# Retention scan and sorted experts on one core: values scaled two steps ahead, loads issued earlier, the first expert chosen sooner, the tail's order changed

## The chip, the cores and the metric

One core of one Trainium2 chip runs the whole program. The metric is the device time of one execution in microseconds. The kernel before took 504.29 us (median of 3 runs, 504.11 to 505.67). All times below are of that kernel.

## What is computed

Two stages. The first is a linear attention with decay (retention), 4 batches x 8 heads x 768 positions x 64 channels; the second sends each of the 3072 resulting rows of 512 channels through the one of 8 experts that scores highest.

```python
for t in range(S):
    state = gamma * state + einsum('bhd,bhe->bhde', k[:, :, t], v[:, :, t])
    y[:, :, t] = scale * einsum('bhd,bhde->bhe', q[:, :, t], state)
x = y.transpose(0, 2, 1, 3).reshape(B * S, H * D)
logits = x @ w_gate
e_idx = argmax(logits, axis=1)
gate_w = softmax(logits)[arange(N), e_idx]
eom = sigmoid(x @ w_output_gate)
for e in range(E):
    mask = e_idx == e
    h = maximum(x[mask] @ w1[e], 0.0)
    out[mask] = gate_w[mask, None] * eom[mask, e, None] * (h @ w2[e])
```

## The kernel before, in words

The scan is cut into 12 steps (`NP`; `LAST` is 11) of 256 positions of one batch, two chunks of 128 each. Positions are taken in order, so after step j the first 256 (j+1) rows exist. The order of TensorE, ScalarE (ACT), VectorE (DVE), GpSimd (POOL) and SyncE (SP) is written out by hand (line 198): each engine runs its instructions in the order of the program text, and waits only for what it needs.

`load(j)` (L220) issues the DMAs of q, k and v of a step on SP: `qn`, `kn` and `vn`, 1.5 MB, into buffers that later hold expert weights (`whi`, eight buffers, for k and v; `wlo`, eight, for q). `prep_v(j)` (L271) multiplies the values of a step by the decay on POOL and writes `vs` (three buffers). In step j TensorE does: the products of the masked scores `am` with `vs[j]` (`values`), the state sums of step j+1 (`sums`, from `vs[j+1]` and `kn[j+1]`), copied to SBUF by ScalarE (`copy_s`), reads of the state with q (`read`), the turning of k and q of step j+2, the scores of step j+1 (`scores`), which VectorE masks at the end of the step (`masked`, L326), and the passage of the finished rows of step j-1 to token order, with the gate products (`tokens`, L388).

Each step also routes the rows of two steps before: VectorE finds the best expert (`route1`, L408), TensorE counts (`count`, L466), VectorE works out each row's place (`route2`, L481) and its gate (`gate1`, `gate2`), ScalarE writes the scaled rows (`rows`, L456), POOL adds row numbers (`marks`, L450) and sends the rows to their places in a sorted DRAM table `srt` by two indirect DMAs (`scatter`, L518), a step later.

To begin the experts early, a first expert is picked when the counts of `PICK` + 1 steps are known (`choose`, L537; `chosen`, L542, loads its number into a register of SP). Its first 256 rows (`HEAD`), which stand in the table after step 7 (`EARLY`; if there are fewer, `early` sets `late`, and the rows are done at the kernel's end by the odd blocks), are loaded by `head_load` (L553), split into a high and a low part by `head_prep` (L563), and run through this expert while the scan ends: a generator (`head_all`, L606) yields after each matmul, and `run_head(n)` (L625) places the next n of them, 12 for the first product of a slice of weights (`head_stage1`, L578) and 12 for the second. The weights come in slices: `load_weights(s)` (L149, three buffers `raw`, one of them shared with the loaded rows) and `split_weights(s)` (L160: high part by ScalarE, low part by two subtractions, one on VectorE, one on POOL for the first eight slices).

After step 11 VectorE ranks the experts by their totals (the order chain, L857 to L884) and sends pad rows (`pads`, L886); the rest of the first expert's rows is loaded when all rows have landed (`load_x`, L942, waits for `settled`), and the expert stage (L1046) runs the remaining rows, then the seven other experts, slice by slice: 12 matmuls for `stage1`, 12 for `stage2`. There the order of VectorE, ScalarE and SP is left to the compiler; TensorE's and POOL's is written out.

The start of a step of the loop:

```python
if j >= 2:
    load(j + 3) if j + 3 < NP else None
if j == 7:
    chosen()
for s in w_at.get(j, ()):
    load_weights(s)
if j >= 3:
    scatter(j - 3)
if j > 1:
    prep_v(j + 1)
```

Of the kernel before, what the change touches and what calls it, by code (L numbers as in the profile page):

```python
# [10 lines left out]
F32 = mybir.dt.float32  # L11
# [20 lines left out]
def retention_moe_kernel(  # L32
# [14 lines left out]
    nc = tc.nc  # L47
# [7 lines left out]
    NDC = DM // P  # L55
    NF = DF // P
# [103 lines left out]
    def split_weights(s: int):  # L160
        raw = raws.pop(s)
        hi = wpool.tile([P, 2, DM], F32R, name="whi", tag="whi")
        lo = wpool.tile([P, 2, DM], F32R, name="wlo", tag="wlo")

        def perm(t):

            return t[:, 1].rearrange("p (dc a j) -> p a dc j", a=4, j=32)

        r2 = raw[:, 1].rearrange("p (a dc j) -> p a dc j", a=4, j=32)
        nc.scalar.copy(hi[:, 0], raw[:, 0])  # L170
        nc.scalar.copy(perm(hi), r2)  # L171
        nc.vector.tensor_sub(lo[:, 0], raw[:, 0], hi[:, 0].bitcast(F32))  # L172
        (nc.gpsimd if s < NF else nc.vector).tensor_sub(perm(lo), r2, perm(hi).bitcast(F32))
        wts[s] = (hi, lo)
# [15 lines left out]
    with ExitStack() as actx:  # L190
# [341 lines left out]
        PICK = 4  # L532
# [30 lines left out]
        def head_prep(g):  # L563
# [12 lines left out]
            (nc.gpsimd if g else nc.vector).tensor_sub(hd["xl"][:, 2 * g:2 * g + 2], tp, hd["xh"][:, 2 * g:2 * g + 2].bitcast(F32))  # L576

        def head_stage1(f):  # L578
# [3 lines left out]
            for r, ls in (("xh", (hi, lo)), ("xl", (hi,))):  # L582
                for dc in range(NDC):
                    for l in ls:
                        nc.tensor.matmul(ps, l[:, 0, dc * P:dc * P + P], hd[r][:, dc], start=(n == 0), stop=(n == 3 * NDC - 1))
                        n += 1
                        yield
# [4 lines left out]
            hd["h", f] = h  # L592

# [107 lines left out]
        w_at = {7: (0,), 8: (1, 2), 9: (3,)}  # L701
        s_at = {8: (0,), 9: (1,)}

        for j in range(1, LAST - 1):
            if j >= 2:
                load(j + 3) if j + 3 < NP else None
            if j == 7:
                chosen()
            for s in w_at.get(j, ()):
                load_weights(s)  # L710
            if j >= 3:
                scatter(j - 3)
            if j > 1:
                prep_v(j + 1)
# [42 lines left out]
            if j >= 2:  # L757
                rows(j - 2)
            tokens(j - 1, 2)
# [4 lines left out]
        scatter(j - 3)  # L764
        prep_v(j + 1)
        head_load()
        for s in (4, 5):
            load_weights(s)
# [13 lines left out]
        split_weights(2)  # L782
# [6 lines left out]
        copy_y(j)  # L789
        gate2(j - 2)  # L790
        route2(j - 2)
        tokens(j - 1, 2)
# [7 lines left out]
        copy_x(j - 1, 1)  # L800
        route1(j - 1)
        marks(j - 1)
        gate1(j - 1)
        tokens(j, 2, st_all)
        split_weights(3)

        j = LAST
        for s in (6,):
            load_weights(s)
# [7 lines left out]
        gate2(j - 2)  # L817
        copy_x(j - 1, 0)
        copy_x(j - 1, 1)
        head_prep(0)  # L820
        issue(read(j, 0, 1), read(j, 1, 0))
        copy_y(j)
        head_prep(1)
        route2(j - 2)
        scatter(j - 3)
        rows(j - 2)
        scatter(j - 2)
        hd["ps"] = pair(1, "h0")
# [5 lines left out]
        gate2(j - 1)  # L834
# [3 lines left out]
        route2(j - 1)  # L838
        run_head(12)
        route1(j)  # L840
        marks(j)
        rows(j - 1)
        scatter(j - 1)
        split_weights(4)
        load_weights(7)
        gate1(j)
# [8 lines left out]
        run_head(24)  # L855
# [12 lines left out]
        nc.vector.tensor_scalar(out=ck, in0=cr, scalar1=1.0 / E, scalar2=float(SLOTS), op0=ALU.mult, op1=ALU.min)  # L868
        ef8 = sm.tile([P, E], F32, name="ef8", tag="ef8")
# [24 lines left out]
        split_weights(6)  # L894
# [3 lines left out]
        settled = list(sent)  # L898
        nc.vector.tensor_copy(n_pad, cum[:, E:E + 1])
# [7 lines left out]

        no = sm.tile([P, 1], F32, name="no", tag="no")
# [12 lines left out]
        split_weights(7)  # L921
# [277 lines left out]
```

## Time and profile before

| what | us |
|---|---|
| median of 3 runs | 504.29 |
| the profiled execution | 505.92 |
| its span | 503.9 |
| TensorE busy (matmuls) | 429.4 |
| VectorE busy | 256.4 |
| ScalarE busy | 201.6 |
| GpSimd busy | 174.4 |

The span is the profiled execution without the 2.0 us around it. Engines overlap, so the busy times do not add up; PE is TensorE's matmul row. A matmul's end is modelled, so a full row means a steady stream and not TensorE at its peak. Idle time of an engine is listed with what ended it.

### The profile page before, as it was taken

Reading aid. Unit: us, or ns where it says so; the run is one execution under the profiler, and the core shown is the slowest. Engines: PE = TensorE matmul, PEld = TensorE weight load, DVE = VectorE, ACT = ScalarE, POOL = GpSimd, SP = SyncE. Lnnn points to the kernel's source line nnn. Section 1 sums busy time; section 2 is a strip of 40 time slices with the busy share of each in tenths; the row PEclk is TensorE's granted clock in tenths of the full one; section 3 lists DMA queues with packets and bytes.
Section 4 is the critical chain, followed back from the end, with each engine's and each line's share of the span. In section 5 each row is a group of like instructions: output and inputs, shape, how many; then the busy total and the mean of one; then the engine's idle time right before and its main releaser. Section 6 shows DMA issues by size and latency. Waiting matters only on the chain.

```text
span 503.9 us, 13073 instructions
## 1 busy us (share of the span) xinstructions
PE 429.4 (85%) x5117; PEld 411.1 (82%) x5119; DVE 256.4 (51%) x711; ACT 201.6 (40%) x416; POOL 174.4 (35%) x221
## 2 busy tenths in 40 slices
PE   6888867667684766769999999999999999999991
PEld 3677766666673766769999999999999999999991
DVE  2416434353542867437547547547556565575111
ACT  2345544434543545015534335335334344353111
POOL 5363233333224246203231034244144243341532
PEclk9999888879876878879999999999999999999997
DMA  9999998357113143292783384485494564841101
GB/s 171 197 239 207 254 251 187 87 141 200 32 57 86 54 161 127 86 195 85 242 203 111 125 205 132 136 220 159 129 224 144 152 192 151 209 156 40 35 24 63
DMA packets 126345, 73.88 MB, mean 147 GB/s; under 512 B 55989, under 2 KB 114873, under 8 KB 126272
## 3 DMA queue, kind: packets, MB, share of 16 engines
q1 hardware_dynamic: 119696, 59.37, 47.4%
q0 software_dynamic: 5536, 13.26, 7.6%
q8 instruction: 42, 0.69, 0.6%
q10 hardware_dynamic: 1040, 0.31, 0.4%
q14 instruction: 31, 0.25, 0.2%
HBM read 59.70 MB, written 13.70 MB: 146 GB/s over the span
## 4 chain that ended last, share of the span: by engine, by line
PE 57%; issue 13%; POOL 9%; DMA 8%; DVE 5%; SPq 4%; ACT 3%; POOLq 0%; ACTq 0%; DVEq 0%
PE h L980 23%; PE a L999 22%; PE py L313 4%; DMA srt<-row,posi 4%; POOL vs L274 3%; SPq L228 3%; POOL out_dram L177 2%; POOL srt L507 2%; PE st L313 2%; PE sc L313 1%; PE pk L301 1%; DMA gb<-in_dec_q_dram 1%; PE px L395 1%; DMA xl<-srt 1%; DMA vn<-in_v_dram 1%
## 5 line engine op out<-in xcount | busy, mean ns | idle before, releaser
L177 POOL DMA_INDIRECT out_dram<-ot,idi x84 | 82.5, 982 | 156.7 <-ACT hh L984 126.9
L980 PE MATMUL h<-xh,whi 128*128 128x224 f32 (+7 forms) x256 | 86.4, 337 | 1.6 <-issue 1.6
L999 PE MATMUL a<-hl,whi 128*128 128x224 f32 (+7 forms) x256 | 85.8, 335 | 0.5 <-DVE hl L985 0.5
L980 PE MATMUL h<-xw,whi 128*128 128x224 f32 (+7 forms) x256 | 86.1, 336 | 0.0
L980 PE MATMUL h<-xh,wlo 128*128 128x224 f32 (+7 forms) x256 | 86.1, 336 | 0.0
L999 PE MATMUL a<-hh,whi 128*128 128x224 f32 (+7 forms) x256 | 85.8, 335 | 0.3 <-ACT hh L984 0.3
L999 PE MATMUL a<-hh,wlo 128*128 128x224 f32 (+7 forms) x256 | 85.7, 335 | 0.0
L172 DVE TENSOR_TENSOR wlo<-raw,whi 128x512 fp32r<-128x512 f32 x64 | 43.9, 687 | 57.7 <-ACT whi L170 49.8
L313 PE MATMUL st<-vs,kn 64*64 64x64 f32 x704 | 39.1, 253 | 36.7 <-POOL vs L274 36.2
L985 DVE SCALAR_TENSOR_TENSOR hl<-h,hh 128x224 fp32r<-128x224 f32 (+7 forms) x64 | 35.0, 546 | 61.2 <-ACT hh L984 61.1
L313 PEld LDWEIGHTS st<-vs,kn 64*64 64x64 f32 x704 | 32.6, 161 | 40.2 <-POOL vs L274 37.9
L984 ACT ACTIVATE hh<-h 128x224 fp32r<-128x224 f32 (+7 forms) x64 | 31.0, 485 | 85.4 <-PE h L980 85.4
L170 ACT CAST whi<-raw 128x512 fp32r<-128x512 f32 x64 | 39.5, 618 | 62.3 <-PE a L999 47.2
L980 PEld LDWEIGHTS h<-xh,whi 128*128 128x128 f32 x256 | 49.0, 191 | 2.1 <-issue 1.8
L980 PEld LDWEIGHTS h<-xw,whi 128*128 128x128 f32 x256 | 49.1, 192 | 0.3
L980 PEld LDWEIGHTS h<-xh,wlo 128*128 128x128 f32 x256 | 49.0, 191 | 0.2
L999 PEld LDWEIGHTS a<-hl,whi 128*128 128x128 f32 x256 | 48.2, 188 | 1.1 <-DVE hl L985 0.7
L999 PEld LDWEIGHTS a<-hh,whi 128*128 128x128 f32 x256 | 48.2, 188 | 0.9 <-ACT hh L984 0.5
L999 PEld LDWEIGHTS a<-hh,wlo 128*128 128x128 f32 x256 | 48.2, 188 | 0.5
L369 ACT COPY sx<-st 128x256 f32<-128x256 f32 x44 | 16.4, 373 | 72.6 <-PE st L313 70.8
L507 POOL DMA_INDIRECT srt<-row,posi x24 | 25.0, 1040 | 46.1 <-DVE am L330 25.6
L171 ACT CAST whi<-raw 128x512 fp32r<-128x512 f32 x64 | 39.5, 617 | 0.0
(187 smaller groups left out, 723.6 us busy)
## 6 DMA issues: line engine op xcount, KB each, us to landing
raw<-in_moe_w_dram SPq DMA_DIRECT2D x128, 256.0 KB
qn<-in_q_dram SPq DMA_DIRECT2D x12, 512.0 KB
kn<-in_k_dram SPq DMA_DIRECT2D x24, 256.0 KB
vn<-in_v_dram SPq DMA_DIRECT2D x24, 256.0 KB
xl<-srt SPq DMA_DIRECT2D x12, 211.2 KB
xl<-srt SPq DMA_DIRECT2D x12, 195.0 KB
out_dram<-ot,idi POOLq DMA_INDIRECT x84
xl<-srt SPq DMA_DIRECT2D x4, 227.5 KB
```

Of the source, the lines that this page charges most:

```text
L170: nc.scalar.copy(hi[:, 0], raw[:, 0])
L171: nc.scalar.copy(perm(hi), r2)
L172: nc.vector.tensor_sub(lo[:, 0], raw[:, 0], hi[:, 0].bitcast(F32))
L177: st = nc.gpsimd.indirect_dma_start(out=dst, out_offset=bass.IndirectOffsetOnAxis(ap=idx, axis=0), in_=src, in_offset=None, bounds_check=n ...
L228: nc.sync.dma_start(t[:, w], chunks(src, j)[:, w * P:(w + 1) * P].rearrange("h p d -> p h d"))
L313: nc.tensor.matmul(o, l, m, start=s, stop=True, skip_group_check=True)
L369: nc.scalar.copy(t, st)
L507: ins = nc.gpsimd.indirect_dma_start(out=srt, out_offset=bass.IndirectOffsetOnAxis(ap=idx, axis=0), in_=src, in_offset=None, bounds_check= ...
L980: nc.tensor.matmul(ps[:, 0:C], l[:, 0, w], r[:, dc, 0:C], start=(n == 0), stop=(n == 3 * NDC - 1))
L984: relu = nc.scalar.activation(hh, ps[:, 0:C], AF.Relu)
L985: nc.vector.scalar_tensor_tensor(out=hl, in0=ps[:, 0:C], scalar=0.0, in1=hh.bitcast(F32), op0=ALU.max, op1=ALU.subtract)
L999: mm = nc.tensor.matmul(accs[d][:, 0:C], l[:, 1, w], r, start=(f == 0 and n == 0), stop=(f == NF - 1 and n == 2))
```

## The change

`vs` of step j+2 is made at the start of step j, ahead of the sends, where that of step j+1 was made behind them. `load(j+4)` stands where `load(j+3)` stood. The first expert is picked one step earlier, and the loads and splits of its weights move with it; for slices 4 to 7 both subtractions of a split run on VectorE. The rows of step 7 are sent at the end of step 9. The second half of the head's low part goes from POOL to VectorE. In the last two steps and in the tail `head_prep`, `gate2`, `rows`, `scatter`, the splits and the head's matmuls stand in other places; the activation and the low part behind the 12th matmul of `head_stage1` are now placed with that matmul and not with the next one.

```diff
--- before.py
+++ after.py
@@ -170,7 +170,7 @@
         nc.scalar.copy(hi[:, 0], raw[:, 0])
         nc.scalar.copy(perm(hi), r2)
         nc.vector.tensor_sub(lo[:, 0], raw[:, 0], hi[:, 0].bitcast(F32))
-        (nc.gpsimd if s < NF else nc.vector).tensor_sub(perm(lo), r2, perm(hi).bitcast(F32))
+        (nc.gpsimd if s < 4 else nc.vector).tensor_sub(perm(lo), r2, perm(hi).bitcast(F32))
         wts[s] = (hi, lo)
 
     def send(dst, idx, src, n):
@@ -529,7 +529,7 @@
             nc.vector.max_index(out=by, in_max=top, in_values=key)
             return top
 
-        PICK = 4
+        PICK = 3
         EARLY = 7
 
         hd = {}
@@ -573,7 +573,7 @@
                 dc = 2 * g + j
                 nc.vector.transpose(tp[:, j].rearrange("p (n i) -> p n i", i=32), t[:, :, dc * 32:dc * 32 + 32])
             nc.scalar.copy(hd["xh"][:, 2 * g:2 * g + 2], tp)
-            (nc.gpsimd if g else nc.vector).tensor_sub(hd["xl"][:, 2 * g:2 * g + 2], tp, hd["xh"][:, 2 * g:2 * g + 2].bitcast(F32))
+            nc.vector.tensor_sub(hd["xl"][:, 2 * g:2 * g + 2], tp, hd["xh"][:, 2 * g:2 * g + 2].bitcast(F32))
 
         def head_stage1(f):
             hi, lo = wts[f]
@@ -584,12 +584,14 @@
                     for l in ls:
                         nc.tensor.matmul(ps, l[:, 0, dc * P:dc * P + P], hd[r][:, dc], start=(n == 0), stop=(n == 3 * NDC - 1))
                         n += 1
-                        yield
+                        if n < 3 * NDC:
+                            yield
             h = hpool.tile([P, 2, HEAD], F32R, name="h0", tag="h0", bufs=3)
             nc.scalar.activation(h[:, 0], ps, AF.Relu)
             nc.vector.scalar_tensor_tensor(out=h[:, 1], in0=ps, scalar=0.0, in1=h[:, 0].bitcast(F32),
                                            op0=ALU.max, op1=ALU.subtract)
             hd["h", f] = h
+            yield
 
         def head_stage2(f):
             hi, lo = wts[f]
@@ -698,20 +700,19 @@
         load(3)
         load(4)
 
-        w_at = {7: (0,), 8: (1, 2), 9: (3,)}
-        s_at = {8: (0,), 9: (1,)}
+        w_at = {6: (0,), 7: (1,), 8: (2,), 9: (3, 4)}
+        s_at = {7: (0,), 8: (1,), 9: (2,)}
 
         for j in range(1, LAST - 1):
-            if j >= 2:
-                load(j + 3) if j + 3 < NP else None
-            if j == 7:
+            if j + 4 < NP:
+                load(j + 4)
+            if j == PICK + 3:
                 chosen()
             for s in w_at.get(j, ()):
                 load_weights(s)
+            prep_v(j + 2)
             if j >= 3:
                 scatter(j - 3)
-            if j > 1:
-                prep_v(j + 1)
             if j == 2:
                 last_consts()
             if j >= 2:
@@ -756,16 +757,15 @@
                 choose() if j - 2 == PICK else early()
             if j >= 2:
                 rows(j - 2)
+            if j == EARLY + 2:
+                scatter(j - 2)
             tokens(j - 1, 2)
             for s in s_at.get(j, ()):
                 split_weights(s)
 
         j = LAST - 1
-        scatter(j - 3)
-        prep_v(j + 1)
         head_load()
-        for s in (4, 5):
-            load_weights(s)
+        load_weights(5)
         copy_x(j - 2, 0)
         new_y(j, 0)
         av = {(w, u): values(j, w, u) for w, u in ((0, 1), (1, 1), (1, 0), (0, 0))}
@@ -779,16 +779,16 @@
         copy_s(j + 1, 1, 0)
         route1(j - 2)
         marks(j - 2)
-        split_weights(2)
         sc = scores(j + 1, 1)
         issue(sums(j + 1, 1, 0), sc[1][0:8])
         copy_s(j + 1, 1, 1)
         issue(read(j, 0, 1), read(j, 1, 0))
         gate1(j - 2)
         count(j - 2)
-        copy_y(j)
         gate2(j - 2)
         route2(j - 2)
+        copy_y(j)
+        split_weights(3)
         tokens(j - 1, 2)
         rows(j - 2)
         issue(sc[0][0:8], sc[1][8:16])
@@ -798,15 +798,16 @@
         masked(j + 1)
         copy_x(j - 1, 0)
         copy_x(j - 1, 1)
+        tokens(j, 2, st_all)
+        head_prep(0)
         route1(j - 1)
         marks(j - 1)
         gate1(j - 1)
-        tokens(j, 2, st_all)
-        split_weights(3)
+        gate2(j - 1)
+        scatter(j - 2)
 
         j = LAST
-        for s in (6,):
-            load_weights(s)
+        load_weights(6)
         new_y(j, 0)
         av = {(w, u): values(j, w, u) for w, u in ((0, 1), (0, 0), (1, 0), (1, 1))}
         issue(av[0, 1], av[0, 0])
@@ -814,36 +815,34 @@
         issue(read(j, 0, 0), read(j, 1, 1))
         touch(j)
         count(j - 2)
-        gate2(j - 2)
+        head_prep(1)
         copy_x(j - 1, 0)
         copy_x(j - 1, 1)
-        head_prep(0)
+        route2(j - 2)
         issue(read(j, 0, 1), read(j, 1, 0))
+        rows(j - 2)
         copy_y(j)
-        head_prep(1)
-        route2(j - 2)
-        scatter(j - 3)
-        rows(j - 2)
         scatter(j - 2)
+        split_weights(4)
         hd["ps"] = pair(1, "h0")
         run_head(12)
         tokens(j, 2)
         route1(j - 1)
         marks(j - 1)
         gate1(j - 1)
-        gate2(j - 1)
         copy_x(j, 0)
         copy_x(j, 1)
         count(j - 1)
         route2(j - 1)
+        gate2(j - 1)
         run_head(12)
+        rows(j - 1)
+        scatter(j - 1)
         route1(j)
         marks(j)
-        rows(j - 1)
-        scatter(j - 1)
-        split_weights(4)
+        gate1(j)
         load_weights(7)
-        gate1(j)
+        run_head(12)
         gate2(j)
         run_head(12)
         rows(j)
@@ -852,7 +851,6 @@
         totals(j)
         scatter(j)
         split_weights(5)
-        run_head(24)
 
         io_ = sm.tile([P, E], F32, name="io_", tag="io_")
         nc.vector.scalar_tensor_tensor(out=io_, in0=first, scalar=-float(16 * NT), in1=io8, op0=ALU.mult, op1=ALU.add)
@@ -866,6 +864,7 @@
         nc.vector.tensor_sub(cr, cr, ordf)
         ck = sm.tile([P, E], F32, name="ck", tag="ck")
         nc.vector.tensor_scalar(out=ck, in0=cr, scalar1=1.0 / E, scalar2=float(SLOTS), op0=ALU.mult, op1=ALU.min)
+        run_head(24)
         ef8 = sm.tile([P, E], F32, name="ef8", tag="ef8")
         nc.vector.scalar_tensor_tensor(out=ef8, in0=ordf, scalar=float(SLOTS), in1=ck, op0=ALU.mult, op1=ALU.add)
         pc = sm.tile([P, E], F32, name="pc", tag="pc")
@@ -891,11 +890,12 @@
             nc.vector.tensor_tensor(out=si, in0=sl, in1=ix, op=ALU.add)
             to_srt(si, zrow, OV, last)
 
-        split_weights(6)
         run_head(24)
         pads(pidx[:, 0:1], False)
         pads(pidx[:, 1:2], False)
         settled = list(sent)
+        split_weights(6)
+        run_head(24)
         nc.vector.tensor_copy(n_pad, cum[:, E:E + 1])
         np_ = nc.values_load(n_pad[0:1, 0:1], engines=(ET.Pool, ET.DVE), min_val=0, max_val=OV)
         with tc.If(np_ > 2 * P):
@@ -905,6 +905,8 @@
         for r in range(1, E):
             rank_e[r] = nc.values_load(order[0:1, r - 1:r], engines=(ET.SP,), min_val=0, max_val=E - 1)
 
+        split_weights(7)
+        run_head(24)
         no = sm.tile([P, 1], F32, name="no", tag="no")
         tj = sm.tile([P, E], F32, name="tj", tag="tj")
         nc.vector.tensor_scalar(out=tj, in0=cnts, scalar1=-float(SLOTS), scalar2=0.0, op0=ALU.add, op1=ALU.max)
@@ -918,7 +920,6 @@
         nc.vector.tensor_reduce(out=on, in_=ck, axis=AX.X, op=ALU.add)
         nc.vector.tensor_add(no, no, on)
         nc.vector.tensor_add(n_odd, no, late)
-        split_weights(7)
         run_head(1000)
```

## Rows read from the trace of the kernel before

A row of a timeline is: start in us, duration in us, engine, line, operation, what it writes and reads, and in brackets the engine's idle time before it with what ended that. A row of rows 2 is: from and to, length, then busy us (with the instructions) of PE, PEld (weight loads), DVE, ACT and POOL, the granted TensorE clock, the busy share of the DMA engines and GB/s. A row of rows 3 is: who waited for whom, us in total, times, the longest.

**Rows 1.** TensorE's busy tenths in 40 slices of the span

```profile
PE   6888867667684766769999999999999999999991
```

**Rows 2.** Windows: steps 4, 7, 9 and 10, the tail, the expert stage

```profile
67.53:80.86 13.33, 10.14 (x274) 9.62 (x274) 6.14 (x28) 6.17 (x14) 4.44 (x6) 0.88 1.09 240
...
109.50:124.04 14.54, 11.38 (x275) 10.54 (x275) 6.27 (x28) 6.30 (x14) 4.39 (x6) 0.81 0.92 237
...
140.89:158.29 17.40, 10.93 (x277) 10.40 (x277) 6.72 (x33) 7.49 (x17) 5.54 (x7) 0.79 0.09 32
158.29:172.13 13.84, 12.27 (x273) 11.16 (x273) 8.53 (x39) 5.86 (x16) 1.80 (x5) 0.71 0.33 80
172.13:224.04 51.91, 35.20 (x346) 33.23 (x345) 32.28 (x137) 18.33 (x45) 18.64 (x21) 0.84 0.48 139
224.04:503.90 279.86, 268.45 (x1548) 265.51 (x1548) 150.25 (x275) 109.46 (x208) 93.68 (x95) 0.98 0.49 141
```

**Rows 3.** Waits of TensorE: steps 2 to 10, then the tail

```profile
PE st L313 <- POOL vs L274: 33.4, 8, 6.7
...
PE h L585 <- DVE h L590: 8.8, 4, 4.0
```

**Rows 4.** Timeline of POOL at the edge of steps 5 and 6

```profile
84.02 0.21 POOL L454 COPY row<-ef 128x8 f32<-128x8 f32 x1 [3.08 <-DVE ef L422]
91.02 1.02 POOL L507 DMA_INDIRECT srt<-row,posi  x1 [6.79 <-DVE am L330]
...
93.36 1.91 POOL L274 TENSOR_TENSOR vs<-vn,gv 128x1024 f32<-128x1024 f32 x1
```

**Rows 5.** Timeline of TensorE, first matmul of step 6

```profile
95.33 0.37 PE L313 MATMUL st<-vs,kn 64*64 64x64 f32 x1 [3.94 <-POOL vs L274]
```

**Rows 6.** Timeline of VectorE in step 5

```profile
84.29 0.17 DVE L432 TENSOR_TENSOR j<-lg,oh 128x16 f32<-128x16 f32 x1
...
85.33 0.17 DVE L437 TENSOR_SCALAR se<-se 128x2 f32<-128x2 f32 x1
86.70 0.16 DVE L445 SCALAR_TENSOR_TENSOR den<-ez,se 128x2 f32<-128x2 f32 x1 [1.20 <-ACT ez L443]
...
89.22 1.28 DVE L330 TENSOR_TENSOR am<-sc,mask 128x512 f32<-128x512 f32 x2
```

**Rows 7.** Timelines of POOL and of VectorE in the tail

```profile
191.32 1.28 POOL L173 TENSOR_TENSOR wlo<-raw,whi 128x512 fp32r<-128x512 f32 x1
...
197.37 2.57 POOL L173 TENSOR_TENSOR wlo<-raw,whi 128x512 fp32r<-128x512 f32 x2
...
190.69 1.95 DVE L437 TENSOR_SCALAR se<-se 128x2 f32<-128x2 f32 x1
...
197.15 2.83 DVE L858 SCALAR_TENSOR_TENSOR io__3323<-first,io 128x8 f32<-128x8 f32 x1
```

**Rows 8.** Timeline of SP's DMA issues: q of steps 5 and 10

```profile
39.21 1.08 SPq L222 DMA_DIRECT2D qn<-in_q_dram  x1
...
76.85 1.17 SPq L222 DMA_DIRECT2D qn<-in_q_dram  x1
```

**Rows 9.** The costliest groups: VectorE's half of a split (line engine op, busy, mean ns)

```profile
L172 DVE TENSOR_TENSOR wlo<-raw,whi 128x512 fp32r<-128x512 f32 x64 | 43.9, 687 | 57.7 <-ACT whi L170 49.8
```

**Rows 10.** Timelines of the tail: totals, pads, load, first use, low part, expert stage

```profile
194.19 0.16 DVE L479 COPY cnts<-misc 128x8 f32<-128x8 f32 x1
...
204.64 1.00 POOL L507 DMA_INDIRECT srt<-zrow,si  x1 [4.70 <-DVE sc L889]
...
210.18 1.99 SPq L947 DMA_DIRECT2D xl<-srt  x4
...
217.05 0.17 DVE L961 CAST idi<-xl 128x7 int32<-128x7 f32 x1 [2.86 <-DMA xl<-srt]
...
219.79 0.42 DVE L590 SCALAR_TENSOR_TENSOR h<-h,h 128x256 fp32r<-128x256 f32 x1
...
224.04 0.52 PE L980 MATMUL h<-xh,whi 128*128 128x224 f32 x1 [1.58 <-issue]
```

## The prediction, made before the changed kernel ran

> **What bounds the kernel now.** I read the busy slices first, then cut the span into the twelve steps of the scan, then asked who TensorE waits for, and last followed single instructions at one step's edge. The slices show two regimes [rows 1]: in its first 18 slices TensorE is busy four to eight tenths, from then on it is full. Cut by step [rows 2], the expert stage from 224.04 to the end is 279.86 us with 268 us of TensorE work; no edit touches it, so I carry it over unchanged. What can move is the 224 us ahead of it: the steps (13 to 17 us each, only about 10 us of it TensorE work) and the tail of 51.9 us from the first matmul of step 11 to the first of the expert stage, with 35 us of TensorE work.
>
> In the steps one wait stands for nearly all of the gap: 33.4 us in 8 pieces, TensorE waiting for the scaled values `vs` [rows 3]. The order on POOL says why [rows 4]. In each step POOL first sends two row blocks of an earlier step (`srt`), which need rows that ScalarE writes at the end of the step, and only then scales the values that the next instruction of TensorE reads: sends from 91.02, `vs` at 93.36 for 1.91 us, and TensorE starts at 95.33 after 3.94 us of nothing [rows 5]. So per step I see some 10.2 us of work and one gap at its edge.
>
> **The change, part by part.**
>
> *Values two steps ahead.* `prep_v(j+2)` now stands ahead of the sends, one step earlier. Its buffer (three of them) is that of step j-1, last read in the first third of that step, so POOL can run it in the middle of step j-1, right behind `marks`, a whole step before TensorE reads it. POOL's work is unchanged: two sends, one scaling, two small copies, 4.4 to 5.5 us a step [rows 2]; nothing that feeds TensorE directly is behind it. The whole 33.4 us go. What is late next? In step 5 the masked scores end at 89.22 + 1.28 = 90.50 [rows 6], while TensorE ran out of work at 95.33 - 3.94 = 91.39 [rows 5]: 0.89 us of slack on VectorE, so TensorE itself is the next bound.
>
> *What the move costs.* The scaling leaves a moment in which VectorE had nothing to do and enters one in which it has. What that can do is seen in the tail: while POOL subtracts from 191.32 to 192.60, an instruction of VectorE of 128x2 elements takes 1.95 us; while POOL subtracts from 197.37, one of 128x8 takes 2.83 us [rows 7], and both end as POOL ends. So I bound the cost per step between nothing (it falls in VectorE's pause) and 1.91 less 0.89, 1.0 us. The new place is behind POOL's copy at 84.02 [rows 4]. VectorE's next are 84.29, then 85.33, then a pause to 86.70 in which it waits for ScalarE [rows 6]; a scaling from 84.4 to 86.3 lies mostly in that pause. I take 0.4 us, nearer the pause, for 8 steps: +3.2 us.
>
> The Trainium skill (SBUF — State Buffer, Who interferes with whom) says the port pair that the two engines share is an exclusive lock for the whole instruction, and that a VectorE instruction with two SBUF inputs contends with a GpSimd one that reads SBUF. The two rows agree with it; by that rule taken alone every step would pay 1.0 us, 8 in all instead of 3.2, which is the first rival below.
>
> *Loads four ahead.* From 39.21 to 76.85 SP issued five steps' loads, 7.5 us each [rows 8], so it already runs ahead of the steps, held by DMA and by free buffers rather than by its place in the order. Moving `load` to j+4 adds no DMA and removes none. With 10.2 us steps TensorE consumes more slowly than 7.5 us; two sends per step (0.5 MB) come between, at the 237 to 240 GB/s of steps 4 and 7 [rows 2] about 2.2 us, sum 9.7. Taken as hidden; if that cover is gone, a step is paced at up to 12 us, 1.8 more.
>
> *Choice from four steps' counts.* The register load on SP now waits one step earlier, and behind it stand the weights of the first expert and `load(11)`, as before. TensorE needs nothing of it for two steps: nothing. The counts of the reference's own inputs give the same expert (7) after four steps, with 146 rows, as after five, with 185, so the expert stage is the same.
>
> *Splits one step earlier, 4 to 7 off POOL.* A split is two casts on ScalarE and two subtractions, of 0.69 us each on VectorE [rows 9], or one there and one of 1.28 us on POOL [rows 7]. Before, POOL's half stood ahead of the sends and `vs` in two steps and made the longest waits (6.7 us [rows 3]); that is already inside the 33.4. Behind the change it is ahead of a `vs` that has a step to spare.
>
> *Clock.* TensorE's granted clock was 0.81, 0.79 and 0.71 in steps 7, 9 and 10, at times the lower of its two levels (1.2 and 2.4 GHz), and the same matmuls were 11.4, 10.9 and 12.3 us busy against 10.1 in step 4 [rows 2]. They follow the waits of rows 3. Without those I give back 3.0 of those 4.2 us.
>
> So step 11 begins 33.4 + 3.0 - 3.2 = 33.2 us earlier, at about 139.
>
> *The tail.* Two chains run through it. The order chain: totals at 194.19, pads sent from 204.64, rest of the first expert's rows loaded from 210.18, expert stage from 224.04 [rows 10]. On it the blocked 2.83 us becomes 0.17 (-2.7), as POOL has no subtraction there; split 6 goes behind the pads (-0.7) and the second half of split 5 comes onto VectorE (+0.7). Ahead of totals, the blocked 1.95 us becomes 0.17 (-1.8), and the head's low parts now leave VectorE right behind their last matmul instead of behind the next step's routing; half of `head_prep` is done a step earlier, while split 4's two subtractions and the second half of `head_prep` come on (+2.1). I take -1.0 for all this beyond the lock, between -4 (TensorE waited 8.8 us for those low parts [rows 3]) and +2. Pads: 5.5 us earlier than before, counted from step 11. From 204.64 to 224.04 it was 19.4 us: 5.5 to landing, 6.9 to the load's first use at 217.05, then the head's last low part at 219.79 behind the preparation of these rows, 2.2 of matmuls, 1.6 to the start. If the head is done by then, the stage starts some 7.8 us after the counterpart of 210.18 (6.9 and one preparation, 0.9 by estimate) instead of 13.9, 6.1 less; if its last low part stays behind the preparation, nothing. I take 2.7, just under the middle, as VectorE's order there is not written out. Tail: -8.2 us.
>
> **Sum.** The profiled execution took 505.92 us (span 503.9 and 2.0 around it), 1.6 above the median of 504.29. 505.92 - 33.2 - 8.2 = 464.5; less 1.6 it is 462.9, so **463 us**.
>
> **Rivals.**
> 1. *VectorE becomes the bound*: `vs` blocks it each step where it counts. For: rows 7. Against: the pause in rows 6. Price 1.0 a step in place of 0.4, and in steps 8 to 10, where POOL's half of a split runs just ahead, some 1.3 more each: 463 + 4.8 + 3.9 = 472. Chance 0.18.
> 2. *Loads become the bound*: 12 us in steps 3 to 8, 1.8 x 6 = 11 us: 474. Against: `load(10)`'s first part was issued at 76.85 [rows 8], before step 5 began, for use in step 8. Chance 0.07.
> 3. *The tail keeps its length*, because what POOL loses VectorE gains (two more half splits and a head part ahead of totals): 471. Chance 0.13.
> 4. *Slower*: choosing after four steps picks an expert with under 256 of the first 2048 rows. Then the flag `late` sends the kernel through the odd blocks at its end: two blocks, each with a load of its rows (6.9 us as in rows 10), one expert's 4.2 MB (17.5 us at 240 GB/s) and some 40 matmuls at the tail's 0.10 us (35.2 us for 346 [rows 2]), 4 us: an estimate of 2 x 28 = 57, so 520 us. It decides at 256: four of the eight experts have fewer by then in the reference's inputs (230 to 252), but the chosen one has 271. Chance 0.03.
> 5. *It does not do what it says*: `vs` still ends last, since a buffer or the landing of the values holds POOL until the step's end. The sends, not a buffer, ended POOL's wait in rows 4. Time as before. Chance 0.02.
>
> **Numbers.** The forecast has 0.57 and spans 455 (stage starts with the head done, no lock cost) to 471. The range to 478 takes in rivals 1 to 3 with the upper end of the lock cost. A measurement tells 0.3% (1.5 us) from no change; faster 0.95, same 0.02 (rival 5), slower 0.03 (rival 4).
>
> **What would show it.** In the changed kernel TensorE's wait for `vs` should be under 3 us in steps 3 to 10 and those steps 10 to 11 us; the masked scores should end at most 1 us after TensorE runs dry. VectorE instructions of 0.17 us that take over 1 us, beside POOL's `vs`, would show the lock, and their place whether it costs. Waits for `vn`, `kn` or `qn` by POOL, TensorE or VectorE would show rival 2. Pads should be sent some 27 us behind step 11's start (32.5 before), and the expert stage start 43 to 44 us behind it; its length should be 279 to 281 us. I am wrong if steps stay over 12 us or if the expert stage itself lengthens.

## The result and the profile after

The changed kernel took **469.92 us** (median of 4 runs, 467.40 to 472.11) beside 504.64 us for the kernel before: ratio 0.931, 95% interval 0.925 to 0.936. The forecast was 463 us in a range of 455 to 478. Two later measurements of the same kernel (e7 and e12 below) gave 466.02 us (464.20 to 466.64; ratio 0.918, 0.914 to 0.923) and 468.23 us (460.07 to 470.30). In the last of them four of six runs lie over 1.5% above the fastest and count as slow, so its ratio is left aside, and medians of all runs stand below. The profiled execution took 471.10 us, span 468.9.

TensorE's slices, beside [rows 1]: the part that is not full is 16 slices long instead of 18, and fuller.

```profile
PE   7988759789877987999999999999999999999991
```

The windows, beside [rows 2]: the nine steps 2 to 10 together, of them the longest (step 4) and a short one (step 8), then the tail and the expert stage. Columns: stretch, length, busy time (instructions) of PE, PEld, DVE, ACT, POOL, granted clock, DMA share, GB/s.

```profile
39.96:145.90 105.94, 85.81 (x2519) 78.01 (x2518) 72.07 (x270) 60.09 (x139) 43.73 (x74) 0.98 0.72 179
64.99:78.99 14.00, 10.93 (x275) 10.08 (x274) 7.30 (x28) 6.46 (x15) 5.18 (x6) 0.88 1.00 231
112.19:122.58 10.39, 9.32 (x292) 8.52 (x291) 8.26 (x29) 6.47 (x17) 5.92 (x6) 1.00 0.31 106
145.90:186.40 40.50, 32.76 (x345) 31.26 (x344) 28.15 (x146) 16.57 (x41) 11.49 (x15) 0.87 0.44 140
186.40:468.90 282.50, 270.51 (x1548) 266.94 (x1548) 152.17 (x278) 110.45 (x211) 93.97 (x95) 0.97 0.52 145
```

The same nine steps of the kernel before in one window:

```profile
39.44:172.13 132.69, 94.75 (x2520) 88.69 (x2519) 61.36 (x277) 59.72 (x139) 41.31 (x73) 0.85 0.59 144
```

Step 11 begins at 145.90 instead of 172.13, 26.2 us earlier; the tail is 40.50 instead of 51.91, 11.4 shorter; the expert stage is 282.50 instead of 279.86, 2.6 longer. Together 35.0, which is the difference of the spans (503.9 and 468.9). The nine steps hold the same 2519 matmuls (2520 in the window before, which cuts one more), yet these were busy for 85.81 us instead of 94.75, at a granted clock of 0.98 instead of 0.85. The single steps are 10.31 to 14.00 us long, and four of the nine are over 12.

TensorE's waits in the steps (36 to 146 us), beside [rows 3]. Columns: who waited for whom, us in total, times, longest.

```profile
PE py L313 <- issue: 10.3, 22, 2.0
PE sc L313 <- issue: 2.9, 2, 2.8
PE misc L472 <- DVE acc L426: 1.9, 2, 1.0
PE px L395 <- issue: 1.8, 1, 1.8
PE misc L471 <- DVE oh L424: 1.0, 2, 0.6
```

The 33.4 us for `vs` are gone. In their place stands a wait that names no other engine: "issue", time in which TensorE waited for nothing that the profile shows, 15.0 us in 25 pieces. In the kernel before it was 2.5 us over the same steps:

```profile
PE px L395 <- issue: 2.1, 2, 1.8
...
PE pq L286 <- issue: 0.2, 1, 0.2
PE py L313 <- issue: 0.2, 1, 0.2
```

POOL's timeline, beside [rows 4]: the scaling of a later step's values runs from 95.64, the sends come 6 us later, and neither holds TensorE. VectorE's timeline beside it shows what the scaling holds: an instruction of 128x8 elements that starts 0.01 us behind it takes 1.90 us and ends as it ends. The same instruction takes at most 0.17 us in the steps of the kernel before, and of all the small routing instructions there only one, in step 10 beside POOL's half of a split, takes over 0.6 us (1.25).

```profile
95.64 1.89 POOL L274 TENSOR_TENSOR vs<-vn,gv 128x1024 f32<-128x1024 f32 x1
101.84 1.47 POOL L507 DMA_INDIRECT srt<-row,posi  x1 [4.32 <-DVE am L330]
```

```profile
95.65 1.90 DVE L426 TENSOR_TENSOR acc<-acc,oh 128x8 bf16<-128x8 bf16 x1
```

The tail's timelines, beside [rows 10]: totals, pads, the load of the remaining rows, the last matmul of the head, first use of the rows, the expert stage.

```profile
164.77 0.16 DVE L479 COPY cnts<-misc 128x8 f32<-128x8 f32 x1
...
173.25 0.97 POOL L507 DMA_INDIRECT srt<-zrow,si  x1 [5.03 <-DVE sc L888]
...
178.89 0.92 SPq L948 DMA_DIRECT2D xl<-srt  x2
...
183.77 0.28 PE L603 MATMUL a<-h,wlo 128*128 128x256 f32 x1
...
185.45 0.13 DVE L962 CAST idi<-xl 128x7 int32<-128x7 f32 x1
...
186.40 0.37 PE L981 MATMUL h<-xh,whi 128*128 128x224 f32 x1 [2.35 <-ACT xh L968]
```

Pads go 27.35 us behind step 11's start (32.5 before), the load 32.99 (38.05 before), and from the load to the expert stage it is 7.51 us instead of 13.86. The head's last matmul (183.77) is done before the rows come into use (185.45), so TensorE now waits for the preparation of these rows.

### The profile page after: what moved, and what is told of

It is laid out like the page before. It is cut to its first block, busy times and chain, and to the rows that moved or that the text cites. A ratio compares the mean times of both kernels' runs of the same rounds, so it can differ in the third digit from the quotient of the medians.

```text
span 468.9 us, 13070 instructions
## 1 busy us (share of the span) xinstructions
PE 422.5 (90%) x5117; PEld 402.6 (86%) x5119; DVE 264.9 (56%) x716; ACT 201.2 (43%) x416; POOL 169.0 (36%) x216
## 4 chain that ended last, share of the span: by engine, by line
PE 48%; issue 7%; DMA 5%; DVE 4%; POOL 3%; ACT 1%; SPq 1%; POOLq 0%; DVEq 0%; ACTq 0%
PE a L1000 24%; PE h L981 24%; DMA srt<-row,posi 3%; POOL out_dram L177 3%; DMA xl<-srt 2%; SPq L948 1%; DVE xw L969 0%; ACT row L460 0%; PE h L585 0%; SPq L153 0%; DVE xt L574 0%; DVE wlo L172 0%; SPq L157 0%; DVE wlo L173 0%; DVE acc L496 0%
## 5 line engine op out<-in xcount | busy, mean ns | idle before, releaser
L172 DVE TENSOR_TENSOR wlo<-raw,whi 128x512 fp32r<-128x512 f32 x64 | 44.0, 687 | 56.6 <-ACT whi L170 46.5
L173 DVE TENSOR_TENSOR wlo<-raw,whi 128x512 fp32r<-128x512 f32 x60 | 41.0, 684 | 0.0
L313 PE MATMUL st<-vs,kn 64*64 64x64 f32 x704 | 33.2, 227 | 2.8 <-POOL vs L274 1.8
```

Of the source, the lines that this page charges most:

```text
L173: (nc.gpsimd if s < 4 else nc.vector).tensor_sub(perm(lo), r2, perm(hi).bitcast(F32))
L313: nc.tensor.matmul(o, l, m, start=s, stop=True, skip_group_check=True)
```

## The experiments

Two theories were tried for the "issue" waits: the indirect sends slow TensorE's instruction supply; or its instruction fetches are late while DMA is full. Beside them: what the single move of the values is worth, what POOL's lock on VectorE costs, and the parts that the prediction costed at nothing. Times are medians of 4 executions (e1 to e8) or 6 (e9 to e12); each run has one profile.

**e1: the values alone, on the kernel before.**

```diff
+            prep_v(j + 2)
             if j >= 3:
                 scatter(j - 3)
-            if j > 1:
-                prep_v(j + 1)
...
         scatter(j - 3)
-        prep_v(j + 1)
         head_load()
```

> The kernel before, with the scaling of the values moved two steps ahead and put ahead of the sends, and nothing else. Theory 'values': this one move carries the whole gain of the steps. TensorE's wait for vs falls from 36 us to under 4, step 11 begins 24 to 28 us earlier than 172.1, the tail keeps the length it had (50 to 53 us), so 477 to 482 us. Rival 'the early loads and the moved splits carry part of it': step 11 begins less than 18 us earlier, 486 us or more. In either case TensorE's gaps of over 0.35 us ahead of weight loads that wait on no semaphore should grow from 3.7 us in the steps to over 12, if the sends cause them and the wait for vs only hid them before.

478.48 us (476.09 to 480.61; ratio 0.946, 0.939 to 0.953) beside 505.9. Windows of the steps and of the tail, and the waits:

```profile
39.02:144.51 105.49, 84.23 (x2519) 77.63 (x2518) 71.54 (x283) 61.21 (x142) 42.96 (x75) 0.96 0.73 182
144.51:196.02 51.51, 35.10 (x346) 33.04 (x345) 30.62 (x130) 16.72 (x42) 17.66 (x20) 0.86 0.47 138
...
PE py L313 <- issue: 9.3, 7, 2.0
PE sc L313 <- issue: 3.8, 3, 1.6
PE px L395 <- issue: 1.7, 2, 1.5
```

Step 11 begins 27.6 us earlier, the tail keeps its length (51.51), TensorE waits for `vs` nowhere, and the issue waits are there. In the profiles of the changed kernel step 11 begins 26.2 us (the first), 34.6 (e7) and 30.5 us earlier (e12), so this one move carries the gain of the steps as far as single profiles can tell.

**e2: the values put back, all else as changed.**

```diff
-            prep_v(j + 2)
             if j >= 3:
                 scatter(j - 3)
+            if j > 1:
+                prep_v(j + 1)
...
         j = LAST - 1
+        prep_v(j + 1)
         head_load()
```

> The changed kernel with the scaling of the values put back behind the sends, one step ahead; loads, choice, splits and tail stay as changed. Theory 'values': the wait for vs returns with 28 us or more, step 11 begins at 168 to 174 and the time is 492 to 498 us, the rest of the change being worth 7 to 12 us, nearly all in the tail. Rival 'the rest carries part of the steps': under 486 us. TensorE's gaps without a semaphore should fall back from 22 us to under 8, since the sends lie in the wait for vs again.

497.29 us (496.19 to 498.99; ratio 0.984, 0.977 to 0.991): 1.6% less, clear of no change. Waits of TensorE, 36 to 170.5 us:

```profile
PE st L313 <- POOL vs L274: 35.2, 8, 6.7
PE px L395 <- issue: 1.8, 1, 1.8
```

The wait is back, and of the issue waits 1.8 us are left: they show only where TensorE has no other wait to hide them. The rest of the change is worth 8.6 us by itself (505.9 to 497.29). By its profile the steps give 1.7 of that, the tail 12.8 (39.07 us instead of 51.91), and the expert stage takes 4.8 back.

**e3: a third send. e4: the sends later in the step.**

```diff
...
                 scatter(j - 3)
+                to_srt(oob, zrow, OV + NT)
+                sent.pop()
```

```diff
-            if j >= 3:
-                scatter(j - 3)
...
                 gate1(j - 2)
+            if j >= 3:
+                scatter(j - 3)
             turn_k(j + 2, 1)
```

> The changed kernel with a third indirect send behind each pair in the loop, all of whose indices are out of range, so that it moves nothing; it costs POOL about 1.3 us a step, and POOL has over 4 us of room in each. Theory 'sends starve TensorE's instruction supply': while POOL builds a send's descriptors TensorE gets its instructions in bursts; a third send adds 0.6 to 1.3 us of gaps to each of 7 steps, the gaps fall beside all three sends, and the time rises by 4 to 8 us. Rival 'the gaps belong to places in TensorE's code, or to the bytes that the sends move': the gaps stay where they are, the time stays within 1.5 us of the changed kernel.

> The changed kernel with the two sends of a step put behind the marks of the order and the first part of the gate in POOL's order, so that they start later in the step. Theory 'sends starve the instruction supply': the gaps follow the sends to their new place, their sum stays at 1 to 1.7 us a step, and the time stays within 3 us of the changed kernel. Rival 'the gaps belong to a place in TensorE's code': they stay at the same instructions of the step.

466.23 us (465.08 to 469.71) and 465.43 us (464.03 to 466.34). The changed kernel itself was not run beside them. POOL's timeline in e3 shows the three sends of a step:

```profile
113.08 1.01 POOL L509 DMA_INDIRECT srt<-row,posi  x1 [0.16 <-POOL vs L276]
114.40 0.98 POOL L509 DMA_INDIRECT srt<-row,posi  x1 [0.30 <-issue]
115.69 0.98 POOL L509 DMA_INDIRECT srt<-zrow,oob  x1 [0.30 <-issue]
```

Both times lie at or under the lower end of the changed kernel's three medians (466.0 to 469.9), where the theory had e3 4 to 8 us above. Gaps of over 0.35 us between TensorE's weight loads, where the later one waits for no semaphore, sum to 14.4 us in e3 and 12.3 in e4, against 17.7 in the first profile and 16.0 in e7 below; ten remain in each, and at 113 to 117 us, beside the three sends, there is none. So the sends are not the cause of the long gaps. These stayed at the same instructions, as the rival said; which these are is shown below.

**e7: the changed kernel again, as base. e5: loads paced. e6: the scaling in halves. e8: keys and values in runs of 512 bytes.**

```diff
...
-                load(j + 4)
+                ld = load(j + 4)
+                if j >= 2:
+                    after(ld, [msk[j]])
```

(`msk[j]` is the masking of the scores; `after` lets an instruction wait for it.)

```diff
-            nc.gpsimd.tensor_mul(vs[j].rearrange("p w h d -> p (w h) d"), vn.pop(j).rearrange("p w h d -> p (w h) d"),
-                                 gv[:, c:c + 2].rearrange("p c h -> p (c h)").unsqueeze(2).broadcast_to([P, 2 * H, D]))
+            n = vn.pop(j)
+            for w in range(2):
+                nc.gpsimd.tensor_mul(vs[j][:, w], n[:, w], gv[:, c + w].unsqueeze(2).broadcast_to([P, H, D]))
```

```diff
-                    nc.sync.dma_start(t[:, w], chunks(src, j)[:, w * P:(w + 1) * P].rearrange("h p d -> p h d"))
+                    nc.sync.dma_start(t[:, w].rearrange("p h d -> p (h d)").rearrange("p (h y) -> p h y", h=H // 2),
+                                      chunks(src, j)[w * H // 2:(w + 1) * H // 2].rearrange("h (p r) d -> p h (r d)", r=2))
```

> The changed kernel once more, unaltered, as the base for the runs beside it. Every theory expects its time again within 0.5% (467.5 to 472.5 us), and gaps of 15 us or more between TensorE's instructions that wait for no semaphore. If the short gaps beside the sends were a property of this code they are there again at the sends; if TensorE's instruction fetches under full DMA make the gaps, each long one ends 1 to 2 us behind the end of a 16 KB fetch.

> The changed kernel with each load four steps ahead held back until the masked scores of the present step are done, so that the loads are spread evenly over the steps in place of running ahead as far as buffers allow; the bytes are the same. Theory 'full DMA delays the instruction fetches of TensorE': in steps 2 to 6 the DMA share falls from 1.0 to about 0.8, the gaps without a semaphore there fall by half (from some 13 to 6 us), and the time falls by 2 to 5 us. Rival 'loads are the bound': spread out they come late, waits for qn, kn or vn appear on VectorE, TensorE or POOL, and the time rises by 2 us or more. If the gaps have nothing to do with the load of the DMA engines, neither.

> The changed kernel with the scaling of the values in two instructions of half the size. Theory 'lock': VectorE's small instructions with two operands from SBUF that stood behind one scaling for up to 1.9 us stand for at most 1.0; TensorE's waits of 0.9 us for the count's sums in steps 5 and 6 go, and the time falls by 0.5 to 2 us. If the lock costs nothing on the path, it stays within 1 us.

> The changed kernel with the keys and values read in runs of 512 bytes in place of 256, the same bytes and the same number of transfers; the heads and rows of both are mixed by it, so that a different computation of the same shape is done, and the counts of the experts, and with them the length of the expert stage, may differ: only the steps are compared. Theory 'full DMA delays the instruction fetches': the packets of keys and values halve, the DMA share in steps 2 to 6 falls from 1.0 to 0.6 or 0.7, the gaps without a semaphore in the steps fall from 15 to 18 us to under 8, and step 11 begins 5 to 9 us earlier, near the 139 of the forecast. Rival 'TensorE runs out of instructions whatever the DMA does': the gaps stay over 12 us and step 11 begins at 141 or later. Rival 'sends': the gaps beside the sends stay, the long ones go.

e7: 466.02 us, under the expected 467.5 to 472.5; e5: 466.60 (463.66 to 474.44); e6: 467.03 (465.01 to 467.85); e8, another computation of the same shape of which only the steps are compared: 463.90 (461.99 to 467.21). Windows of e7 (steps 2 to 10, then four steps, and one of the four):

```profile
39.37:137.50 98.13, 81.56 (x2519) 75.20 (x2519) 69.32 (x270) 60.17 (x139) 43.70 (x74) 0.98 0.78 196
...
50.38:94.20 43.82, 35.47 (x1116) 32.84 (x1115) 29.83 (x119) 25.28 (x60) 19.66 (x22) 1.00 0.98 239
...
74.01:84.66 10.65, 8.87 (x293) 8.21 (x293) 7.88 (x32) 6.17 (x16) 2.10 (x3) 1.00 0.92 226
```

The same four steps and the same single step in e8:

```profile
53.09:92.30 39.21, 34.80 (x1115) 32.52 (x1114) 31.24 (x119) 24.73 (x60) 16.15 (x18) 0.98 0.64 183
...
73.10:83.09 9.99, 8.63 (x294) 8.15 (x293) 7.05 (x32) 6.23 (x16) 3.07 (x5) 1.00 0.18 60
```

TensorE's fetches can be followed in the trace's list of DMA packets: 42 packets of 16 KB of the kind "instruction" on one queue in an execution. That they are TensorE's is read from their number: one for every 246 of its 10 311 instructions, and no other engine has 1000. The gaps beside them (us from the span's start):

```
kernel  gap from   long   until    16 KB fetch      from its end to the gap's end
after     48.33    1.85   50.19    47.76 to 48.84   1.35
after     59.50    2.84   62.34    59.70 to 61.01   1.33
after     68.42    2.12   70.54    67.90 to 69.08   1.46
e7        52.21    2.36   54.57    51.77 to 53.31   1.26
e7        98.66    2.14  100.80    98.31 to 99.34   1.46
e8        92.62    3.31   95.93    93.30 to 94.49   1.44
e8        none                     76.83 to 77.77
e8        none                     80.30 to 81.32
e8        none                     84.71 to 85.63

DMA share in the 3 us before a fetch   under 0.3   0.3-0.6   0.6-0.9   over 0.9
fetches in the steps, 12 profiles          59         27        33        111
of them with a gap of over 0.9 us           3          2        10         66
```

The table of shares takes all profiles with the values two steps ahead, and the fetches from 44 us to step 11. Of the 83 gaps of over 0.9 us in them, 81 end 1.2 to 1.9 us behind the end of such a fetch, and these follow 66 of 111 fetches under full DMA but 5 of 86 where the share was under 0.6. Counted along TensorE's instructions (weight loads, matmuls and its sequencer's waits), the long gaps stand on a grid: every 256th instruction, to within two. In seven profiles whose order on TensorE is the same, 47 of 49 gaps of at least 0.8 us lie on it, at any step and with the sends anywhere; only their length differs from run to run ("-" is none):

```
instruction  1984 2240 2496 2752 3008 3264 3520 3776 4032 4288 4544 5056
after         1.9    -  2.8  2.1    -    -  0.8  1.0    -    -    -    -
e3            2.9    -  2.0  2.7    -    -  1.3    -    -  1.1  1.7  1.0
e4            1.2    -    -  3.4  1.0    -  1.3    -    -  1.5  1.6    -
e5            2.1    -  1.9  1.9  1.0    -  1.4    -  0.8    -  3.2    -
e7            2.5  2.4  0.8  1.3  1.8    -  1.2    -    -  1.0  2.1  1.0
e8            2.7    -    -    -  1.0  1.5    -    -    -  3.3  1.6    -
e12           1.9  1.0  1.9  2.1  2.6  2.0  1.1    -    -  2.5    -    -
```

e6 tells the count from the place in the program: its twelve further waits on TensorE's sequencer move the gaps up to four weight loads earlier, and they stay on the 256th instructions.

The trace also shows what is late. From TensorE's first instruction of one such block of 256 to the start of the fetch that the next block follows, the median is 1.14 us where the DMA share was under 0.3 (59 fetches) and 2.49 us where it was over 0.9 (111). The packet itself takes 1.06 and 1.19 us, and the next block never starts less than 1.20 us behind its end. That adds up to 3.4 and 4.9 us (an estimate from these figures), and TensorE needs about 4 us for a block (75.74 to 79.63 in e8). What holds the fetch back before its start, the trace does not tell.

**So the long issue waits are instruction fetches that come late while DMA is full.** In four of e8's steps the DMA share is 0.64 instead of 0.98, they are 4.6 us shorter and hold two gaps of over 0.9 us instead of four (the next, of 3.31 us, begins 0.3 us behind them). As a whole e8 missed its mark: gaps of 10.6 us (under 8 expected; 16.0 in e7), and step 11 begins at 136.92 against 137.50, because it lost 2.5 us in its first step and 1.6 where weights and the last load come together (92.30 to 106.80).

The Trainium skill (Runtime: NRT & Kernel Launch, Instruction fetch mechanics) says that the sequencer fetches ahead in blocks of 16 KiB (256 instructions) on its own DMA queue and that crossing into the next is mostly hidden. The packets and the grid agree with the block; the gaps behind 66 of 111 fetches disagree with "mostly hidden" where other transfers fill the DMA.

e5 missed too: its gaps are 15.1 us and its time is e7's, since pacing hardly lowered the DMA share of those steps (0.92 against 0.98). It excludes the loads as a bound, no more. e6 shows the lock: the longest blocked `acc` instruction falls from 1.90 to 1.04 us, TensorE's 0.7 us of waiting for `acc` goes, and the time does not fall. Halving shortens each block and does not remove the lock, so e6 shows that the long blocks cost nothing that these runs can tell (those of e7 spread over 2.4 us, those of e6 over 2.8); what the lock costs as a whole it does not show.

**e12: the changed kernel, base of three. e9: subtractions back on POOL. e10: choice from five steps' counts. e11: loads three ahead.**

```diff
-        (nc.gpsimd if s < 4 else nc.vector).tensor_sub(perm(lo), r2, perm(hi).bitcast(F32))
+        (nc.gpsimd if s < NF else nc.vector).tensor_sub(perm(lo), r2, perm(hi).bitcast(F32))
...
-            nc.vector.tensor_sub(hd["xl"][:, 2 * g:2 * g + 2], tp, hd["xh"][:, 2 * g:2 * g + 2].bitcast(F32))
+            (nc.gpsimd if g else nc.vector).tensor_sub(hd["xl"][:, 2 * g:2 * g + 2], tp, hd["xh"][:, 2 * g:2 * g + 2].bitcast(F32))
```

```diff
-        PICK = 3
+        PICK = 4
...
-        w_at = {6: (0,), 7: (1,), 8: (2,), 9: (3, 4)}
-        s_at = {7: (0,), 8: (1,), 9: (2,)}
+        w_at = {7: (0, 1), 8: (2,), 9: (3, 4)}
+        s_at = {8: (0, 1), 9: (2,)}
```

```diff
-            if j + 4 < NP:
-                load(j + 4)
+            if j >= 2:
+                load(j + 3) if j + 3 < NP else None
```

> The changed kernel unaltered, as the base of the three runs beside it: 464 to 472 us, what its two measurements so far span.

> The changed kernel with the second subtraction of splits 4 to 7 and of the second head part back on POOL, as before; order and everything else as changed. Theory 'lock in the tail': some of VectorE's small instructions of routing stand for the length of POOL's subtraction again, 1.95 and 2.83 us as in the kernel before, and as they lie on the way to the totals and the pads, the tail is 2 to 5 us longer than 40.5. Rival 'POOL took work from VectorE that counts': the tail is 0 to 2 us shorter. If those instructions now lie off the path, within 1 us.

> The changed kernel with the first expert chosen from five steps' counts, as before, and the loads and splits of the first three weights one step later to suit; the same expert comes out. Theory of the prediction: nothing but the place of work moves, within 1.5 us of the base, and the step that holds the choice shows TensorE's wait of some 2 us for VectorE one step later. Rival 'the weights' loads lie where DMA is full and starve TensorE of instructions': spread behind the last load of the queries they leave the DMA share of steps 6 and 7 lower, the gaps without a semaphore there (3 us) shrink, and the time falls by 1 to 3 us. Rival 'the weights come late': split 0 or 1 waits, and the tail grows.

> The changed kernel with the loads issued three steps ahead, as before. Theory of the prediction: SP runs ahead of the steps and is held by DMA and by free buffers, so within 1.5 us of the base, with the same waits for qn, kn and vn. Rival 'the steps are now short enough that three steps ahead is late': the scaling of the values, which now comes two steps ahead, waits for vn longer, TensorE waits for vs again, and the time is 3 us or more longer.

Medians 468.23 (e12), 468.85 (e9, 464.46 to 471.42), 467.76 (e10, 463.85 to 468.99), 467.13 (e11, 466.11 to 472.12): none can be told from the base. Choice and loads are worth nothing that shows, as forecast. The rivals of e10 fall: its issue waits in the steps are 13.5 us against 14.7, and its tail is 40.5 us. So does that of e11: TensorE waits for `vs` nowhere in its steps. In e9 VectorE's and POOL's timelines show the lock on the order chain, and e12's the same instruction free:

```profile
162.77 1.76 DVE L859 CAST ordf<-order 128x8 f32<-128x8 uint32 x1
...
163.22 1.28 POOL L173 TENSOR_TENSOR wlo<-raw,whi 128x512 fp32r<-128x512 f32 x1
```

```profile
164.03 0.17 DVE L859 CAST ordf<-order 128x8 f32<-128x8 uint32 x1
```

The tail is 41.88 us in e9, and 40.62 in e12, 40.50 and 40.52 in the two other profiles of the changed kernel: 1.3 longer, under the 2 to 5 expected. That is the lock and the work that VectorE is spared taken together; this run does not part them. No version beat the changed kernel beyond its spread.

## Why the prediction was right, and where by luck

On the profiled execution the forecast was 464.5 us and the time 471.1, 6.6 more: 7.0 in the steps and 2.6 in the expert stage, less 3.2 in the tail (and 0.2 around the span). The prediction named two signs of being wrong, steps of over 12 us and a longer expert stage; both came, in four of nine steps (one of nine in e7) and with 282.50 us, and both are explained below as far as the runs go.

**The values: right.** "The whole 33.4 us go" held in both directions: nothing of the wait is left in e1, and 35.2 us come back in e2. So did "the sends, not a buffer": in the steps 2 to 10 POOL waited for `vn` for 8.5 us in 3 pieces, and TensorE for `vs` nowhere.

**"TensorE itself is the next bound": this step failed.** It asked only what other engines could be late with. Issue waits went from 2.5 to 15.0 us, 12.5 that no term held. In e7, where they went to 13.8, they are late instruction fetches: 15.5 of 16.0 us of the gaps between weight loads lie on the grid. In the first profile only 9.2 of 17.7 do, and the other half stays open (last section). The trace of before hardly showed them, since the wait for `vs` let the fetches catch up (as in e2); but it had one gap of 1.85 us on the grid, at 47.01, and the DMA share of 1.09 in step 4 [rows 2].

**"Some 10.2 us of work" and the clock: mis-sized.** The 10.1 us of step 4, which the prediction took as the undisturbed price, came at a clock of 0.88 itself [rows 2]. Over nine steps the busy time of the matmuls fell by 8.9 us (94.75 to 85.81), and by 13.2 in e7 (81.56), not by 3.0. The granted clock stood at times at the lower of its two levels as long as TensorE ran dry at each step's edge (0.85 on the mean); once it did not, it was 1.00 in eight of the nine steps and 0.88 in step 4.

**The lock: mechanism right, price not borne out.** 3.2 us were taken. All waits for VectorE and ScalarE in the steps together grew from 2.1 to 5.2 us in this profile, and are 2.2 in e7; in e6 shorter blocks bring nothing. So rival 1 falls. One detail of [rows 7] differs from the condition that the prediction gives: the instruction of 1.95 us reads one tile (`se`) from SBUF, not two, and is blocked all the same, as the cast in e9 is.

The terms for the steps: -33.4 + 12.5 + 3.1 - 8.9 = -26.7, by windows 132.69 to 105.94, -26.75. In e7 they are -33.4 + 11.3 + 0.1 - 13.2 = -35.2, by windows -34.6: there step 11 begins at 137.50, by the forecast at 139. Two missed terms of opposite sign stand against each other: 12.5 us of issue waits and 5.9 more from the clock in the first profile, 11.3 and 10.2 in e7. That they nearly cancel in e7 and so bring it near the forecast is luck, and the outcome of the steps differs by 8 us between these two executions.

**The tail: right in its chain, wrong in one choice.** Up to the load it is 5.1 us shorter (5.5 forecast). From there the choice was "2.7, just under the middle" between 6.1 and nothing; it came out 6.35, since the head was done before the rows were there. For what moved from POOL to VectorE it had 4.5 us of lock less up to 2.8 of added work; e9 measures 1.3 for both together, in reach of that difference, and does not test the single terms. Rival 3 falls.

**The expert stage: not unchanged.** It lost 2.6 us (4.2 in e7, 0.6 in e1, 4.8 in e2), so it goes with the new tail and not with the values. In the first profile it lies in the first 36 us, where 236 matmuls were done instead of 250, at a clock of 0.91 instead of 0.95. Which of clock and waits comes first was not tried.

**Rivals 2, 4 and 5.** Loads three ahead cost nothing that shows (e11), though the loads did slow the steps, by way of the fetches. The kernel did not get slower, and the wait for `vs` went, so rivals 4 and 5 fall.

**The range.** Its lower end of 455 is not the sum of what it names: 462.9 less 3.4 (head done) and 3.2 (no lock) is 456.3.

## What to carry to other kernels

When a wait at every step's edge goes, take the price of the work that remains from a stretch at full granted clock, and expect the clock to give back what those waits cost. Then ask what the wait was hiding besides engines: with DMA full, TensorE's instruction fetches came late here, and three in five cost 0.9 to 4.3 us each as soon as no other wait hid them. Where the length of a chain hangs on which of two things is done first, work that out from the rows and choose, and do not take the middle.

## What the runs showed of the hardware

TensorE's instruction fetches (packets of 16 KB on a queue of their own) go with blocks of 256 instructions. Under a DMA share of over 0.9 three in five were followed by a gap of over 0.9 us, under 0.6 one in seventeen. Gaps of up to 4.3 us were seen (e11), ending 1.2 to 1.9 us behind the fetch's end. Halving the number of packets for keys and values (512 bytes instead of 256) took the DMA share of four steps from 0.98 to 0.64.

Open: the first profile of the changed kernel also has sixteen short gaps of 0.35 to 0.6 us, fifteen of them (7.5 us) off that grid and most beside the sends. e7, the same program, has four, one of them off the grid; e3 and e4 exclude the sends as a regular cause, and no run explains them.
